# A DFT's maxima taken in passes, and the last token tiles split on VectorE: one change to a fused FNet and MLP kernel

## Chip, cores, metric

The kernel runs on one core of one Trainium2 chip. The metric is the device time of one execution in microseconds (us), the median of several runs. The core has TensorE (PE, with its weight loads PEld), VectorE (DVE), ScalarE (ACT), GpSimd (POOL) and SyncE (SP), which issues most DMAs.

## What is computed

```python
x = A_x                                    # 1 x 2048 x 576, f32
xn = _layernorm(x)                         # over the 576 columns
a, b = xn @ dft_hid_re.T, xn @ dft_hid_im.T
fourier = dft_seq_re @ a - dft_seq_im @ b  # dft_seq: 2048 x 2048
mlp = maximum(xn @ w1, 0) @ w2             # w1: 576 x 4608, w2: 4608 x 576
return x + fourier + mlp
```

All in float32. The kernel writes each f32 operand as a high and a low f16 part (`split`, or a copy and a subtraction) and multiplies high by high, high by low and low by high. The factors are scaled by powers of two, for which the kernel needs the largest absolute value of each matrix.

## The kernel before

**Tiles.** The 2048 tokens are 16 tiles of 128 rows and 4 groups of 512. The 4608 hidden columns are 9 blocks of 512. Most products are Strassen products in Winograd's form: 7 products instead of 8 for each 2 x 2 partition, which costs sums of blocks on VectorE ahead of and behind TensorE.

**The MLP** is a sequence of 36 steps, counted from 0: `steps[n]` is block n // 4 and group n % 4. Step n computes the first product of its block and group (`run`, L593 and L612 on TensorE) and the second product of the step before (`mlp2`, L699 on TensorE, L710 on ScalarE, L714 on VectorE). What `mlp2` has gathered in a sum buffer is added to a spill in DRAM by a DMA of GpSimd's queue (L717). From block 2 on, the order within a step is a list written out by hand, of which the change touches the entries `more` and `count`.

Two lists fill the gaps of the steps. `todo` holds the preparation of the next block: loads into a ring of two raw buffers, maxima, splits and sums, ten slots to a step (`work`). In the last block (steps 32 to 35) it holds the preparation of the DFT over the columns instead: `load_d(e)` loads one half of its matrix, `max_d` reduces it to a maximum per partition on VectorE (L161), `power_d` makes the scale, `split_d` (L229 on ScalarE, L230 on VectorE) and `sums_d` make the operands. Since the ring holds one half only, half 1 is loaded, reduced, then half 0 is loaded, reduced and split, and half 1 is loaded again. `passes` holds 64 loads of 512 KB of the sequence DFT's matrices into one staging buffer (`first_c`), each followed in the next pass by a sum of absolute values on ScalarE (`sum_c`, L1139). A step takes two passes, a step of group 1 three.

**The DFT over columns** has 8 steps (`for s in range(NS)`): TensorE's products (L1312), their sums, and `convert`, which makes the f16 operands R of four token tiles: copies on ScalarE (L1359, the high parts), subtractions for the low parts (L1363) and differences (L1367, L1375, L1376) on VectorE. Low parts of the later products (`a.start > 2`) are made by GpSimd.

**The last stage** multiplies the sequence DFT's matrices with R, in 16 units `(p, kh)`: p is one of 8 pairs of output tiles, kh says which half of the token tiles is summed over (kh = 0: tiles 0 to 7). Each unit has 7 products of 24 matmuls (L1555); VectorE adds each to the output in SBUF (L1561). An output starts as what the spill holds (`load_out`) and is stored after its kh = 1 unit. The operands of a unit come from four blocks of 512 KB (`load_c`, one unit ahead), with sums on VectorE (L1409 to L1414) and the split (L229, L230) three products ahead. The last 22 operations of `convert` (`rest_r`, two token tiles) are done during the first units, two after each product, their low parts by GpSimd.

TensorE, ScalarE, VectorE, GpSimd and SP each take their instructions in order; `tc.issue_after` puts an instruction behind another one on its engine. All five queues come from one scheduler that follows the order of the program where nothing is waited for.

Of the kernel before, what the change touches and what calls it, by code (L numbers as in the profile page):

```python
# [10 lines left out]
F32 = mybir.dt.float32  # L11
# [7 lines left out]
P = 128  # L19
S = 2048  # L20
D = 576
# [33 lines left out]
def kernel(  # L55
# [103 lines left out]
    def magnitude(dst, src):  # L159

        nc.vector.tensor_reduce(dst, src, AX.XY, ALU.max, apply_absolute_value=True)  # L161
# [61 lines left out]
    def cell(tag, n=NQ):  # L223
        return small.tile([P, n], F32, tag=f"c_{tag}", name=f"c_{tag}", bufs=2)
# [821 lines left out]
            owed.pop()  # L1046
            work(True)

    PARTS_D = (slice(0, 3), slice(3, KT))
    DK = 7  # L1050
    dspots = [dspot[0], w2spots[3][0], kspot[0] + DX + FW]
    dparts = [
# [13 lines left out]
    def load_d(e):  # L1066
        for j in (2 * e, 2 * e + 1):
            load_raw(("d", j), dft[:, :, j * EH : (j + 1) * EH], [P, KT, EH])

    def max_d(j, c):  # L1070

        if "d" not in mx:
            mx["d"] = cell("md", 8)
        k = 2 * j + c
        with tc.issue_after(order["vfree"]):
            magnitude(mx["d"][:, k : k + 1], raws["d", j][:, PARTS_D[c]])

    def power_d():
        m = cell("mdd", 1)
# [35 lines left out]

    NP = NT // 2
    HK = NT // 2
    units = [(0, 0), (1, 0), (1, 1), (0, 1)] + [(p, kh) for p in range(2, NP) for kh in range(2)]
    sums_c = const.tile([P, len(units), 4], F32, name="sums_c")
    firsts = {}  # L1120

# [12 lines left out]
    def sum_c(m):  # L1134

        n, q = divmod(m, 4)
        f = firsts.pop(m)
        with tc.issue_after(order.get("free", order["s"])):
            nc.scalar.activation(  # L1139
                f, f, AF.Abs, scale=2.0**-10, accum_out=sums_c[:, n, q : q + 1]  # L1140
            )


    passes = [
        lambda m=m: (sum_c(m - 1) if m else None, first_c(m)) for m in range(4 * len(units))
    ]
    passes.append(lambda: sum_c(4 * len(units) - 1))

    tq = itertools.chain(*(sums_x(g) for g in range(NG)))
    for n in range(2, len(steps)):  # L1150
        b, g = steps[n]
        pb, pg = steps[n - 1]
        if g == 0 and b:
            if b + 1 < NB:
                todo += prepare_block(b + 1)
            else:
                d = power_d()
                for e in (1, 0):
                    todo += [lambda e=e: load_d(e)] + [lambda: None] * 2
                    todo += [lambda j=j, c=c: max_d(j, c) for j in (2 * e, 2 * e + 1) for c in range(2)]  # L1160
                todo += [lambda: next(d), lambda: None, lambda: later(d)]
                todo += prepare_d(0) + [lambda: load_d(1), lambda: None] + prepare_d(1)[:DA]
        if b == 0 and g + 1 < NG:
            with tc.issue_after(order["lo"]):
                weave(stats([(g + 1) * TG + i for i in range(TG)]))
        if b == NB - 1 and g == 1:

            w = turn("w2s", w2spots)
            sumbufs[:] = [
                w[:, k : k + 2 * EH].rearrange("p (c e) -> p c e", e=EH)  # L1170
                for k in range(0, 6 * EH, 2 * EH)
            ]
        if b >= BB:
            run, rests = step_products(n)
            used = lambda q: run(q, True)
            m = lambda q: mlp2(pb, pg, q)
            end = lambda q: ends and ends.pop(0)()
            ready = lambda q: [work() for _ in range(q)]
            brief = lambda q: [work(True) for _ in range(q)]
            count = lambda q: passes and passes.pop(0)()  # L1180
            left = lambda q: n == 2 * NG and lates[-1][q]()
            t_sum = lambda q: next(tq, None)
            more = lambda q: g == 1 and count(q)
            rest = lambda q: rests(n + 1 if n + 1 < len(steps) else None)
            for do, q in (
                (run, P1), (left, 0), (run, P5), (end, 0), (end, 0), (m, 0), (brief, 1), (left, 1),
                (run, P6), (end, 0), (end, 0), (run, P2), (t_sum, 0), (m, 1), (used, P2), (more, 0), (ready, 1),
                (run, P7), (t_sum, 0), (ready, 1), (m, 2), (used, P7), (count, 0), (m, 3), (brief, 1),
                (rest, 0), (run, P3), (brief, 1), (m, 4), (used, P3), (t_sum, 0), (ready, 1),
                (run, P4), (used, P4), (t_sum, 0), (m, 5), (ready, 1), (count, 0),  # L1190
                (m, 6), (brief, 3),
            ):
                do(q)
            continue
        ps = []
        for i in range(NF):
            if n == 2:
                if i == 3:
                    mlp2(pb, pg, 0)
                    mlp2(pb, pg, 1)  # L1200
                ps.append(early.pop(0) if early else mlp1(b, g, i))
            else:
                if n == 3 and i == 0:
                    mlp2(pb, pg, 0)
                    mlp2(pb, pg, 1)
                with behind("pe" if n == 3 and i == 0 else None):
                    mlp1_step(b, g, i, ps)
            if n == 2:
                t = (g + 1) * TG + i
                normalize(t, after="free" if i == 3 else None)  # L1210
                remainder(t, nc.vector)
                transposes_dma(t, nc.scalar)
            if i % 2:
                after = ("w2hi", ("E", 15))[i // 2] if n == 2 else None
                lates.append(mlp1_out(
                    b, g, i // 2, *ps[i - 1 : i + 1], after=after,
                    late=i == 1 or n == 7 if b else n == 2,
                ))
                if n == 2 and i == 1:
                    lates[-1][0]()  # L1220
            if n > 2 and i == 1:
                gates[n - 2] = order["s"], order["lo"]
            if n == 2:
                if i > 1:
                    todo += prepare_block(1) if i == 2 else []
                    for _ in range(1 if i == 2 else 2):
                        work()
                continue
            if b:
                work()  # L1230
            for q in ((2,), (3,), (4, 5), (6,))[i] if n == 3 else range(2 * i, min(2 * i + 2, 7)):
                mlp2(pb, pg, q)
                if b:
                    if q in (3, 5):
                        lates[-1][q == 5]()
                    for _ in range((2, 0, 0, 5, 0, 0, 2)[q]):
                        next(tq, None)
                else:
                    for _ in range(2):
                        work()  # L1240
            for _ in range(1 + i % 2 if b else (2, 2, 2, 4)[i]):
                work()
            if (n, i) > (6, 1) and i % 2 and passes:
                passes.pop(0)()
        if n == 2:
            for q in range(2, 7):
                mlp2(pb, pg, q)
                if q == 2:
                    lates[-2][1](("E", 15))
                if q in (3, 5):  # L1250
                    lates[-1][q == 5]()

            gates[n - 2] = order["s"], order["lo"]
            for _ in range(9):
                work()
# [96 lines left out]
    def convert(s, k):  # L1352
# [6 lines left out]
            nc.scalar.activation(r[:, 0, a], x[:, b], AF.Copy)  # L1359

        def lo(a, b):
            tt = (nc.gpsimd if a.start > 2 or late_r else nc.vector).tensor_tensor
            tt(r[:, 1, a], x[:, b], r[:, 0, a], ALU.subtract)  # L1363

        def t13():
# [82 lines left out]
    for s in range(NS):  # L1448
        lows = [(s, 0, P4), (s, 0, P3), (s, 1, P4), (s, 1, P3)]
        lows += [(s, e, P2) for e in range(2)]  # L1450
        if s + 1 < NS:
            lows += [(s + 1, e, P5) for e in range(2)]
        end = s == NS - 1
        one, two = convert(s, 1), convert(s, 0)
        if s == 0:
            seq = (
# [49 lines left out]
        if s == 5:  # L1506
            load_c(0, [2, 3, 1])
    outs = {}
    ospots = [(dspots[1], o4 + 2 * W2W)[k] for k in (0, 1, 1, 0)]

    def load_out(p):
        o = outs[p] = words((ospots[p if p < 2 else 2 + p % 2], 4 * EH)).rearrange("p (h e) -> p h e", h=2)
        for h in range(2):
            g, c = divmod(p + h * NP, TG)
            for col in range(2):
                nc.sync.dma_start(o[:, h, col * EH : (col + 1) * EH], spill[g, c // 2, col][:, c % 2])

    psw.release()
    psd = [tc.alloc_tile_pool(name="psd0", bufs=4, space=PSUM, side="right")]
# [11 lines left out]
    AHEAD = 3  # L1531
    load_out(0)
    operand(2, False)
    late_r.append(True)
    keys = ("h1", "l1", "h2", "l2", "t13", "t2", "t4", "h3b", "l3b", "h3a", "l3a")
    rest_r = [d[k] for d in (old, late) for k in keys]
    for n, (p, kh) in enumerate(units):
        if n + 1 < len(units):
            load_c(n + 1)
        if n == 0:  # L1540
            load_out(1)
        elif n > 2 and kh and units[n + 1 :]:
            load_out(units[n + 1][0])
        for i, (q, rq, first, row, col) in enumerate(PRODUCTS):
            m = n * 7 + i
            if m + AHEAD < 7 * len(units):
# [14 lines left out]
            order["o"] = nc.vector.scalar_tensor_tensor(  # L1561
                o, ps, us["c"][:, n : n + 1], o, ALU.mult, ALU.add
            ).ins
            for _ in range(2):
                if rest_r:
                    rest_r.pop(0)()
            if kh and i in (2, 4, 5, 6):
# [58 lines left out]
```

## Time and profile before

| | |
|---|---|
| median of 3 runs | 1237.79 us (1235.23 to 1239.27) |
| the profiled execution | 1238.07 us, span 1235.9 us |
| TensorE busy | 1211.0 us (98% of the span) |
| VectorE busy | 999.4 us (81%) |
| ScalarE busy | 707.2 us (57%) |
| GpSimd busy | 210.2 us (17%) |
| granted TensorE clock | 1.00 |

A line of the waits names the engine and line that waited, the releaser, the total in us, how often, and the longest. A group has its count, then busy us and mean ns, then the idle time just ahead of it and what ended most of that. A line of a timeline has start, length, engine and line, and in brackets the idle time ahead of it.

### The profile page before, as it was taken

To read this page: it belongs to the slowest core of one execution; us is meant where nothing else is said; L and a number is where in the kernel's file an instruction comes from. 1 tells how busy PE (TensorE), PEld (TensorE's weight loads), DVE (VectorE), ACT (ScalarE), POOL (GpSimd) and SP (SyncE) were. 2 spreads that over 40 slices of the span, in tenths; PEclk is the share of its full clock that TensorE was granted. 3 is DMA by queue.
4 is the path that set the end of the run, shared out by engine and by line. 5 is a ranking of instruction groups with operands and counts; after the bars stand their busy time and mean duration, and the time that the engine had idled before them with its cause. 6 is when DMAs were issued, how large, how long until landed. Compare 5 with 4: busy or idle time off the path is not lost.

```text
span 1235.9 us, 24513 instructions
## 1 busy us (share of the span) xinstructions
PE 1211.0 (98%) x10173; PEld 956.2 (77%) x10173; DVE 999.4 (81%) x1619; ACT 707.2 (57%) x1073; POOL 210.2 (17%) x241
## 2 busy tenths in 40 slices
PE   8999999999999999999999999899989999999998
PEld 7665657888888788888888888677767777777777
DVE  8998899778877788778877877777798878787875
ACT  5655457677686666767766757656643333333332
POOL 2431211111121212111111111144440000000000
PEclk9999999999999999999999999999999999999999
DMA  8994545757566567567576686520243534433420
GB/s 316 210 159 99 85 70 134 150 122 161 136 136 155 138 143 154 119 152 145 120 161 155 136 195 128 104 30 1 69 158 110 168 112 137 142 126 125 134 88 20
DMA packets 82207, 160.80 MB, mean 130 GB/s; under 512 B 22320, under 2 KB 42544, under 8 KB 82096
## 3 DMA queue, kind: packets, MB, share of 16 engines
q1 hardware_dynamic: 59312, 116.77, 30.0%
q0 software_dynamic: 22784, 42.48, 23.9%
q8 instruction: 79, 1.29, 0.4%
q14 instruction: 32, 0.26, 0.1%
HBM read 108.10 MB, written 51.90 MB: 129 GB/s over the span
## 4 chain that ended last, share of the span: by engine, by line
PE 73%; DVE 15%; issue 5%; ACT 3%; DMA 3%; POOL 0%; SPq 0%; ACTq 0%; POOLq 0%; DVEq 0%
PE p L1555 24%; PE p L699 22%; PE bank L593 19%; DVE arena L230 3%; PE U L1312 3%; PE W L1312 2%; DMA arena<-in_w_dram 1%; PE p L392 1%; DVE arena L714 1%; PE bank L612 1%; ACT arena L229 1%; DVE arena L468 1%; DMA arena<-in_dft_dram 1%; PE V L1312 1%; DVE arena L451 1%
## 5 line engine op out<-in xcount | busy, mean ns | idle before, releaser
L699 PE MATMUL p<-arena 128*128 128x288 f16 x3024 | 400.2, 286 | 5.8 <-DVE arena L714 5.7
L699 PEld LDWEIGHTS <-arena 128*128 128x128 f16 x3024 | 295.8, 98 | 83.5 <-issue 8.4
L1555 PE MATMUL p<-arena 128*128 128x288 f16 x2688 | 330.2, 286 | 5.2 <-DVE arena L1561 4.7
L1555 PEld LDWEIGHTS <-arena 128*128 128x128 f16 x2688 | 263.0, 98 | 72.4 <-issue 6.3
L593 PE MATMUL bank<-arena 128*128 128x256 f16 x2580 | 304.8, 273 | 1.2 <-ACT arena L647 1.1
L593 PEld LDWEIGHTS <-arena 128*128 128x128 f16 x2580 | 250.1, 98 | 39.1 <-issue 7.6
L229 ACT ACTIVATE arena<-arena,sc_c 128x1024 f16<-128x1024 f32 x112 | 124.3, 1144 | 199.5 <-DVE arena L1410 75.3
L717 POOL DMA_DIRECT2D spill<-arena x144 | 128.6, 911 | 553.4 <-DVE arena L714 504.5
L230 DVE SCALAR_TENSOR_TENSOR arena<-arena,sc_c 128x1024 f16<-128x1024 f32 x112 | 144.3, 1312 | 51.8 <-ACT arena L229 51.8
L710 ACT ACTIVATE arena<-p,c_ub 128x576 f32<-128x576 f32 x144 | 105.5, 734 | 43.3 <-PE p L699 38.2
L230 DVE SCALAR_TENSOR_TENSOR arena<-arena,c_sw 128x640 f16<-128x640 f32 (+2 forms) x118 | 98.2, 847 | 24.8 <-ACT arena L229 24.5
L229 ACT ACTIVATE arena<-arena,c_sw 128x640 f16<-128x640 f32 (+3 forms) x118 | 90.3, 795 | 23.1 <-DVE c_sw L171 10.8
L628 DVE TENSOR_TENSOR arena<-arena 128x1024 f16<-128x1024 f32 x56 | 68.5, 1224 | 42.9 <-ACT arena L624 42.8
L392 PE MATMUL p<-arena 128*128 128x128 f16 (+1 forms) x680 | 98.5, 300 | 1.8 <-ACT arena L347 1.1
L714 DVE SCALAR_TENSOR_TENSOR arena<-p,c_ub,arena 128x576 f32<-128x576 f32 x108 | 87.4, 810 | 7.7 <-PE p L699 5.1
L1312 PEld LDWEIGHTS <-arena 128*128 128x128 f16 x738 | 71.6, 98 | 19.7 <-issue 1.9
L392 PEld LDWEIGHTS <-arena 128*128 128x128 f16 x680 | 52.3, 98 | 40.3 <-issue 3.8
L619 ACT ACTIVATE arena<-arena 128x512 f16<-128x512 f32 x56 | 35.2, 628 | 67.7 <-DVE arena L649 39.7
L1561 DVE SCALAR_TENSOR_TENSOR arena<-p,us_c,arena 128x288 f32<-128x288 f32 x112 | 57.5, 513 | 13.8 <-PE p L1555 13.4
L1139 ACT ACTIVATE arena<-arena 128x1024 f32<-128x1024 f32 x64 | 67.0, 1047 | 2.0 <-DMA arena<-in_cre_dram 1.0
L1363 POOL TENSOR_TENSOR arena<-arena 128x576 f16<-128x576 f32 (+1 forms) x36 | 52.1, 1460 | 60.2 <-ACT arena L1359 52.5
L624 ACT ACTIVATE arena<-arena 128x1024 f16<-128x1024 f32 x56 | 58.8, 1050 | 0.0
(151 smaller groups left out, 1119.7 us busy)
## 6 DMA issues: line engine op xcount, KB each, us to landing
spill<-arena POOLq DMA_DIRECT2D x144, 288.0 KB, 4.8
arena<-in_cre_dram SPq DMA_DIRECT2D x64, 512.0 KB, 4.2
arena<-in_cim_dram SPq DMA_DIRECT2D x64, 512.0 KB, 4.7
arena<-in_w_dram SPq DMA_DIRECT2D x17, 640.0 KB, 5.3
arena<-in_w_dram SPq DMA_DIRECT2D x18, 576.0 KB, 4.8
arena<-in_x_dram SPq DMA_DIRECT2D x16, 288.0 KB, 7.1
spill<-in_x_dram SPq DMA_DIRECT2D x16, 288.0 KB, 5.5
arena<-spill SPq DMA_DIRECT2D x32, 144.0 KB, 2.2
```

The source lines that it names most:

```text
L229: nc.scalar.activation(hi, src, AF.Copy, scale=s).ins,
L230: nc.vector.scalar_tensor_tensor(lo, src, s, hi, ALU.mult, ALU.subtract).ins,
L392: order["m1"] = nc.tensor.matmul(ps[:, cols], w1s[b, i // 2][:, hl, i % 2 * KT + k], xT[g][:, kx, cols], start=(start and n == 0), stop=(s ...
L593: nc.tensor.matmul(ps[:, i], l, r, start=first and i == m == 0, stop=m == len(todo) - 1, skip_group_check=not first or i > 0,)
L628: order["lo"] = nc.vector.tensor_tensor(lo, stage[:, 1 + 2 * i :][:, :2], hi, ALU.subtract).ins
L699: order["pe"] = nc.tensor.matmul(ps[:, c], h[:, x, qa, c * P : (c + 1) * P], w[:, y, qb], start=first and i == 0 and j == 0, stop=i == NQ ...
L710: freed(nc.scalar.activation(o, ps, AF.Copy, scale=us[b]))
L714: add = nc.vector.scalar_tensor_tensor(o, ps, us[b], o, ALU.mult, ALU.add)
L717: nc.gpsimd.dma_start(spill[g, row, col], o, accum_op=ALU.add)
L1139: nc.scalar.activation(f, f, AF.Abs, scale=2.0**-10, accum_out=sums_c[:, n, q : q + 1])
L1312: nc.tensor.matmul(ps, l, r, start=first and m == 0, stop=m == len(todo) - 1, skip_group_check=not first,)
L1555: nc.tensor.matmul(ps, w[:, a, k], r[:, c, RQ[rq]], start=first and k == 0 and j == 0, stop=k == HK - 1 and j == 2, skip_group_check=not f ...
```

## The change

The maxima of the DFT's column matrices are taken in six passes of 960 columns through the staging buffer of `passes`, in front of pass 24, by VectorE. Steps of group 3 now also take three passes. In the last block, half 0 is loaded and split at once and half 1 is loaded one time, four slots ahead of its first split.

The units of the last stage start with four of kh = 0 (p = 0 to 3), and then take kh = 1 of the same four. Two outputs in SBUF don't hold four, so those of p = 0 and 1 are written back to their spill after their first unit and read again. `late_r` is set at the last step of the DFT over columns, and its sense is turned: from there on all low parts are made by VectorE. The 22 operations of `rest_r` are handed out six to a unit.

```diff
+    ND = 6
+
+    def first_d(m):
+        if m == 0:
+            mx["d"] = const.tile([P, ND], F32, name="max_d")
+        n = KT * 2 * D // ND
+        f = firsts["d", m] = words(fspot, n)
+        with behind("loads"):
+            nc.sync.dma_start(f, dft.rearrange("p k e -> p (k e)")[:, m * n : (m + 1) * n])
+
-    def max_d(j, c):
...
+    def max_d(m):
+        f = firsts.pop(("d", m)).rearrange("p (a b) -> p a b", a=2)
         with tc.issue_after(order["vfree"]):
-            magnitude(mx["d"][:, k : k + 1], raws["d", j][:, PARTS_D[c]])
+            magnitude(mx["d"][:, m : m + 1], f)
...
-    units = [(0, 0), (1, 0), (1, 1), (0, 1)] + [(p, kh) for p in range(2, NP) for kh in range(2)]
+    units = [(p, 0) for p in range(4)] + [(p, 1) for p in range(3, -1, -1)] + [(p, kh) for p in range(4, NP) for kh in range(2)]
...
+    parts = [(first_c, sum_c, m) for m in range(4 * len(units))]
+    parts[24:24] = [(first_d, max_d, m) for m in range(ND)]
+
+    def part(k):
+
+        if k:
+            _, take, m = parts[k - 1]
+            take(m)
+        if k < len(parts):
+            load, _, m = parts[k]
+            load(m)
+
+    passes = [lambda k=k: part(k) for k in range(len(parts) + 1)]
...
                 d = power_d()
-                for e in (1, 0):
-                    todo += [lambda e=e: load_d(e)] + [lambda: None] * 2
-                    todo += [lambda j=j, c=c: max_d(j, c) for j in (2 * e, 2 * e + 1) for c in range(2)]
-                todo += [lambda: next(d), lambda: None, lambda: later(d)]
-                todo += prepare_d(0) + [lambda: load_d(1), lambda: None] + prepare_d(1)[:DA]
+                todo += [lambda: (load_d(0), next(d)), lambda: None, lambda: later(d)]
+                todo += prepare_d(0) + [lambda: load_d(1)] + [lambda: None] * 3 + prepare_d(1)[:DA]
...
-            more = lambda q: g == 1 and count(q)
+            more = lambda q: g % 2 and count(q)
...
-            tt = (nc.gpsimd if a.start > 2 or late_r else nc.vector).tensor_tensor
+            tt = (nc.gpsimd if a.start > 2 and not late_r else nc.vector).tensor_tensor
...
         end = s == NS - 1
+        if end:
+            late_r.append(True)
...
-    ospots = [(dspots[1], o4 + 2 * W2W)[k] for k in (0, 1, 1, 0)]
-
-    def load_out(p):
-        o = outs[p] = words((ospots[p if p < 2 else 2 + p % 2], 4 * EH)).rearrange("p (h e) -> p h e", h=2)
+    ospots = [dspots[1], o4 + 2 * W2W]
+
+    def load_out(p, back=False):
+        o = outs[p] = words((ospots[(p + (p > 3)) % 2], 4 * EH)).rearrange("p (h e) -> p h e", h=2)
...
-                nc.sync.dma_start(o[:, h, col * EH : (col + 1) * EH], spill[g, c // 2, col][:, c % 2])
+                part = o[:, h, col * EH : (col + 1) * EH], spill[g, c // 2, col][:, c % 2]
+                nc.sync.dma_start(*(part[::-1] if back else part))
...
-    late_r.append(True)
...
-        if n == 0:
-            load_out(1)
-        elif n > 2 and kh and units[n + 1 :]:
-            load_out(units[n + 1][0])
+        after = units[n + 1 : n + 2]
+        if n in (1, 2):
+            load_out(p - 1, True)
+        if after and after[0][0] != p and n != 4:
+            load_out(after[0][0])
...
-            for _ in range(2):
+            for _ in range((1, 0, 0, 1, 2, 2, 0)[i]):
                 if rest_r:
                     rest_r.pop(0)()
```

More of the change, by code (lines that the diff above doesn't have):

```diff
@@ L1047, in work @@
             work(True)
-    PARTS_D = (slice(0, 3), slice(3, KT))
     DK = 7
@@ L1068, in load_d @@
             load_raw(("d", j), dft[:, :, j * EH : (j + 1) * EH], [P, KT, EH])
-    def max_d(j, c):
-        if "d" not in mx:
-            mx["d"] = cell("md", 8)
-        k = 2 * j + c
+    ND = 6
[8 more added lines that the diff above has]
+        f = firsts.pop(("d", m)).rearrange("p (a b) -> p a b", a=2)
         with tc.issue_after(order["vfree"]):
-            magnitude(mx["d"][:, k : k + 1], raws["d", j][:, PARTS_D[c]])
+            magnitude(mx["d"][:, m : m + 1], f)
     def power_d():
@@ L1141, in sum_c @@
             )
[L1144 to L1147, printed above, removed]
+    parts = [(first_c, sum_c, m) for m in range(4 * len(units))]
[8 more added lines that the diff above has]
+    passes = [lambda k=k: part(k) for k in range(len(parts) + 1)]
     tq = itertools.chain(*(sums_x(g) for g in range(NG)))
```

## The prediction

> **What bounds the kernel now.** I read the page, then what TensorE waited for, then TensorE by stretches of time, then the timelines of the engines around each stretch with a gap.
>
> ```profile
> span 1235.9 us, 24513 instructions
> PE 1211.0 (98%) x10173; PEld 956.2 (77%) x10173; DVE 999.4 (81%) x1619; ACT 707.2 (57%) x1073; POOL 210.2 (17%) x241
> PE p L699 <- DVE arena L714: 5.7, 8, 1.9
> PE p L1555 <- DVE arena L1561: 4.7, 5, 1.5
> PE bank L612 <- DVE arena L649: 3.5, 2, 2.3
> PE p L1555 <- ACT arena L1348: 0.5, 1, 0.5
> ```
>
> TensorE is busy for 1211.0 of 1235.9 us and the change takes no matmul away, so it can only move the 24.9 us in which TensorE stands still. The waits (line, releaser, total, times, longest) show where the touched parts sit: 4.7 us in the last stage (L1555), behind VectorE's additions of L1561. The timelines put 1.07 us (L593) and 2.29 us of the 3.5 (L612) into the end of the MLP. Those 8.1 us are the most that the two aims can bring.
>
> ```profile
> L1555 PE MATMUL p<-arena 128*128 128x288 f16 x2688 | 330.2, 286 | 5.2 <-DVE arena L1561 4.7
> 895.00:905.00 10.00, 8.20 (x66) 6.27 (x65) 9.97 (x9) 5.90 (x9) 6.37 (x4) 1.00 0.87 289
> 905.00:915.00 10.00, 9.14 (x72) 7.03 (x72) 10.00 (x13) 6.20 (x7) 2.96 (x3) 1.00 0.32 111
> 915.00:925.00 10.00, 7.99 (x64) 6.25 (x64) 9.97 (x10) 1.94 (x3) 5.77 (x3) 1.00 0.32 104
> 960.00:970.00 10.00, 10.00 (x84) 7.99 (x82) 8.34 (x9) 2.45 (x3) 0.00 (x0) 1.00 0.42 129
> ```
>
> The first row is the last stage's matmuls: 330.2 us for 112 products, 2.95 us each. The others are stretches: length, then busy time of PE, weight load, DVE, ACT, POOL, then clock, DMA share and GB/s. The first unit and a half of the last stage are the only place where VectorE is full (29.9 of 30 us) and TensorE loses (4.7 us). Later VectorE needs 8.3 of 10 us, GpSimd does nothing, and TensorE loses nothing.
>
> **Low parts of the last token tiles.** Why VectorE is full there shows in the groups of 885 to 921 us (first three) and of 925 to 1200 us (the next two):
>
> ```profile
> L230 DVE SCALAR_TENSOR_TENSOR arena<-arena,sc_c 128x1024 f16<-128x1024 f32 x9 | 14.7, 1652 | 1.1 <-ACT arena L229 1.1
> L1363 POOL TENSOR_TENSOR arena<-arena 128x576 f16<-128x576 f32 x10 | 17.0, 1719 | 17.6 <-ACT arena L1359 17.6
> L1409 DVE TENSOR_TENSOR arena<-arena 128x1024 f32<-128x1024 f32 x1 | 2.3, 2295 | 0.0
> L230 DVE SCALAR_TENSOR_TENSOR arena<-arena,sc_c 128x1024 f16<-128x1024 f32 x94 | 118.3, 1282 | 46.4 <-ACT arena L229 46.4
> L1409 DVE TENSOR_TENSOR arena<-arena 128x1024 f32<-128x1024 f32 x13 | 15.8, 1215 | 0.0
> 883.79 1.13 DVE L1363 TENSOR_TENSOR arena<-arena 128x576 f16<-128x576 f32 x2 [1.36 <-ACT arena L1359]
> ```
>
> The same instruction takes 1282 ns while GpSimd rests and 1652 ns while it works. L230 alone pays 9 x 0.37 = 3.3 us; one L1409 takes 2295 ns, against 1215 later, so another 1.1; the shorter ones take it to an estimated 7 us. The change makes the 12 low parts that GpSimd did in this stretch (10 wide, 2 narrow) VectorE instructions: 4 in the last step of the DFT over columns, 8 in the four units. A wide and a narrow one took 1.13 us together on VectorE (last row), so about 0.7 each: 12 x 0.7 = 8.4 us. VectorE's work in all hardly changes (7 taken, 8.4 given). But only the 4 (about 3 us) must be done early. The other 8, and the differences of L1367 to L1376 between them, are handed out six operations to a unit, because the first four units now read only token tiles 0 to 7. Per unit of 7 products (7 x 2.95 = 20.6 us) VectorE has 20.6 x (1 - 0.834) = 3.4 us free and gets about 2. In the first 40 us it loses 7 us of slowed work and some 2 of moved differences and gets 3 + 1.2 of low parts: 38 of 40 us become about 33, the share at which TensorE loses nothing later.
>
> What is late next: the 0.5 us behind L1348 stays (ScalarE empties PSUM). A product that adds to an older bank needs L1561 of two products before, and after two extra operations in a row VectorE catches up late; I leave 0.8 us for that. Term: 4.7 - 0.8 = **3.9 us gained**. Bounds: 4.7 if nothing stays; 2.0 if each of the four units keeps some 0.7 us, since 2 of the 3.4 us free go in clumps.
>
> Here a rule of the Trainium skill stands against the row. SBUF — State Buffer, section "Who interferes with whom", says that a VectorE instruction with two SBUF inputs and a GpSimd one that reads SBUF exclude each other, for the whole instruction. By it the delay would be up to 12 x 1.7 = 20 us (an estimate from GpSimd's row) instead of 7. The trace shows partial delays; the stall to be gained is 4.7 us either way.
>
> **Order of units and the write-back.** Two partial outputs (4 DMAs of 144 KB each) go back to their spill and are read again, all on SP's queue. Behind the write-back, which waits for L1561 of the unit's last product, stand the reload and the next column loads. The reload is used a whole unit (20.6 us) later, the loads about half a unit later; single loads land in 4 to 11 us (rows below). I take 0. If that cover went, a unit would wait for the landing beyond it, at most about 2 us each, twice.
>
> **DFT loads at the end of the MLP.** Before, the second half of the DFT's matrix is loaded a third time one slot ahead of its use, and ScalarE waits for it:
>
> ```profile
> 767.97 0.55 SPq L141 DMA_DIRECT2D arena<-in_dft_dram  x1
> 770.92 1.01 ACT L229 ACTIVATE arena<-arena,c_sd 128x864 f16<-128x864 f32 x1 [3.46 <-DMA arena<-in_dft_dram]
> 778.64 0.78 ACT L229 ACTIVATE arena<-arena,c_sd 128x576 f16<-128x576 f32 x1 [2.55 <-DMA arena<-in_dft_dram]
> 775.19 1.47 PE L593 MATMUL bank<-arena 128*128 128x256 f16 x12 [1.07 <-ACT arena L647]
> 782.04 0.40 PE L612 MATMUL bank<-arena 64*128 64x256 f16 x4 [2.29 <-DVE arena L649]
> 737.39 0.19 ACT L1139 ACTIVATION_READ_ACCUMULATOR arena<-arena 128x1 f32 x1
> 745.38 2.35 ACT L229 ACTIVATE arena<-arena,c_sd 128x864 f16<-128x864 f32 x3
> 747.64 0.57 ACT L645 ACTIVATE arena<-bank 128x512 f32<-128x512 f32 x1
> ```
>
> ScalarE's copies that free PSUM (L645 to L648) queue behind, then VectorE's L649, then TensorE: 1.07 + 2.29 = **3.4 us that go** in step 35 (steps count from 0; the last block is 32 to 35). With the maxima out of the list, the 12 slots in front of the splits vanish, and by the count of ten slots a step the splits of the first half take step 32 from slot 3, the second load slot 3 of step 33, its first three splits slots 7 to 9 of step 33. Those are the slots of the 745.38 row.
>
> What is new there. (1) SP issues that load behind the pass's own load, and that waits for its sum on ScalarE (737.39 + 0.19 in step 33), so about 738.3 with the maxima's pushes. 512 + 720 + 720 KB go one after the other. In the old place the last piece landed 778.64 - 767.97 = 10.7 us after its issue with the same three in flight: here 749, while the third split wants it at 747. At TensorE, 0 to 2.3 us; I take 0.5, since the second piece goes out 2 us closer to the first than before. If every piece landed in the 2 us plus bytes over 436 GB/s of the Trainium skill (DMA: Bandwidth & Descriptors, "Anatomy of one DMA"), all three would be there after an estimated 6.6 us and this item would be 0; the landings in this trace are longer. (2) The split of rows 15 and 16 now lands in slot 9 of step 32. Its low part overwrites a sum buffer that step 32's last product has just sent to the spill:
>
> ```profile
> 723.63 1.84 POOL L717 DMA_DIRECT2D spill<-arena  x2 [2.03 <-DVE arena L714]
> spill<-arena POOLq DMA_DIRECT2D x3, 288.0 KB, 6.6
> 730.77 1.23 DVE L628 TENSOR_TENSOR arena<-arena 128x1024 f16<-128x1024 f32 x1 [1.55 <-ACT arena L624]
> 732.51 0.81 DVE L714 SCALAR_TENSOR_TENSOR arena<-p,c_ub,arena 128x576 f32<-128x576 f32 x1
> 733.30 3.10 PE L699 MATMUL p<-arena 128*128 128x288 f16 x24
> ```
>
> The second of these DMAs starts at 724.55 and lands 6.6 us later: 731.1. VectorE stands still until then and has the split, another split (0.8 and 1.1), L628, L646 and L714 to do: L714 ends at about 735.5 instead of 733.3, and the second product of the last row starts at 734.8. I take 0.8 us (0 to 1.6). Together this part: 3.4 - 0.5 - 0.8 = **2.1 us gained**, from 3.4 to -0.5.
>
> **Maxima in passes.** The eight reductions go from steps 32 and 33, where they cost nothing:
>
> ```profile
> 700.00:740.00 40.00, 40.00 (x352) 33.20 (x351) 29.34 (x40) 24.83 (x40) 7.25 (x9) 1.00 0.84 196
> L161 DVE TENSOR_REDUCE c_md<-arena 128x1 f32<-128x864 f32 (+1 forms) x8 | 7.2, 895 | 0.0
> 713.52 1.04 DVE L161 TENSOR_REDUCE c_md<-arena 128x1 f32<-128x864 f32 x1
> ```
>
> Six of 960 columns come, 1.04 + 96/960 = about 1.1 us each. Counting passes (3 before step 8, then 10 per block), they fall into steps 17 (three), 18 (two) and 19 (one). New is that VectorE waits for a load which goes out only when the maximum before it is done. Step 17 in the old trace:
>
> ```profile
> 396.40 0.68 DVE L649 TENSOR_TENSOR arena<-bank,arena 128x512 f32<-128x512 f32 x1
> 397.73 0.61 PE L612 MATMUL bank<-arena 64*128 64x256 f16 x8
> 400.81 0.75 DVE L230 SCALAR_TENSOR_TENSOR arena<-arena,c_sw 128x512 f16<-128x512 f32 x1 [1.94 <-ACT arena L229]
> 403.47 0.81 DVE L714 SCALAR_TENSOR_TENSOR arena<-p,c_ub,arena 128x576 f32<-128x576 f32 x1
> 402.81 3.15 PE L699 MATMUL p<-arena 128*128 128x288 f16 x24
> arena<-in_cre_dram SPq DMA_DIRECT2D x1, 512.0 KB, 3.9
> arena<-in_cim_dram SPq DMA_DIRECT2D x1, 512.0 KB, 7.8
> ```
>
> The first maximum stands ahead of L649: it ends 1.1 us later, at 398.2, and L612 wants to start at 397.73: 0.5 us. The load behind it goes out at 397.2 and lands in 3.9 us (the load of this step at 399.6): 401.1, while VectorE, idle from 398.9 before, is there at 400.0. The maximum, the split of 400.81, L650, ScalarE's answer and L632 follow, and L714 ends at 405.6 instead of 404.3; TensorE, itself 0.5 late, needs it at 404.8: 0.8 us. The third, behind a weight load (the 7.8 us row), may reach into step 18: 0.5. Step 18 has VectorE idle where its two fall; step 19 repeats the first case: 0.4. Together **2.2 us lost**, 0.4 (order luckier, landings short) to 5 (every landing 7.8 us). The sums that move to the fourth step of a block are 1 us of ScalarE each, on an engine that is 57% busy: 0.
>
> **Sum.** -3.9 - 2.1 + 2.2 = -3.8 us. The profiled execution took 1238.07 us, 2.2 us around its span: 1234.3. The median shown is 1237.79, 0.28 lower: **1234.0**. A measurement of this kernel can tell about 0.3% (3.7 us) from no change, so the forecast lies right on that bound, at 1234.1.
>
> **Rivals.**
> - *All covers hold* (0.15): the maxima find gaps, the loads land. -4.3 - 3.4 + 0.4 = -7.3: 1230.5. For it: eight reductions cost nothing at 700 to 740. Against it: VectorE had no load to wait for there in the passes' rhythm.
> - *The DFT wait only changes place* (0.18): ScalarE is held by the second load in step 33 (2.3 at TensorE), the sum buffer costs 1.6, the passes 2.5, the units 0.9 more. -3.0 + 0.5 + 2.5 = 0: 1237.8. For it: 10.7 us of landing, and only four slots between issue and use.
> - *VectorE is stopped by the passes' loads* (0.15), the slower side. Where a load lands after about 5 us the maximum comes too late, and it decides from about 8 us on for the second, third and fifth pass: at 8.5 us they hold VectorE for 5, 4 and 2 us, and TensorE nearly as long, since L714 stands behind; with 2 us from the pushes, 13 instead of 2.2: +7, 1244.8 at the worst and 1241.5 with half of it. For it: the 7.8 us row; against it: most such loads land in about 4 us.
> - That the change doesn't do what it says is excluded by the listing: the flag is set before step 7's low parts are issued, and 71 passes fit 73 slots.
>
> **How the numbers follow.** The forecast has 0.52, its own range 1231 to 1236.5; about six tenths of it lies below 1234.1. Faster by over 0.3%: 0.15 + 0.32 = 0.47 and a little of the second rival, 0.49. Slower: 0.15. Same: 0.36. The range leaves out the worst half of the slower rival and the best of the first: 1229.8 to 1240.5.
>
> **What would show it.** Right: no POOL group of L1363 after about 885 us, L230 near 1.28 us throughout, TensorE's wait for L1561 at 1 us or less; no ScalarE wait for the DFT's loads in the last step; reductions of 960 columns in steps 17 to 19 with small gaps at L612 and L699. Wrong: VectorE waiting several us for those loads, ScalarE held in step 33, gaps in units 1 to 4, or a wait for the reloaded outputs.

## The result and the profile after

| | before | after |
|---|---|---|
| median us (9 runs each, taken together) | 1237.85 | 1232.97 |
| lowest and highest | 1235.23, 1239.27 | 1230.92, 1234.5 |
| the profiled execution, its span | 1238.07, 1235.9 | 1233.90, 1232.1 |

The ratio is 0.9959 (95%: 0.9947 to 0.9970). The kernel is 4.9 us faster, which is a little over the 0.3% that can be told from no change. The forecast was 1234.0, 1.0 us too slow.

The page of the kernel after: its head, then the lines of what TensorE waited for (line, releaser, total us, times, longest).

```profile
span 1232.1 us, 24558 instructions
PE 1211.8 (98%) x10173; PEld 957.2 (78%) x10173; DVE 999.3 (81%) x1629; ACT 707.8 (57%) x1073; POOL 189.6 (15%) x229
PE p L699 <- DVE arena L714: 6.6, 8, 2.1
PE bank L612 <- DVE arena L649: 1.2, 1, 1.2
PE p L1570 <- DVE arena L1576: 0.4, 1, 0.4
```

L1570 and L1576 are the last stage's matmul and addition (L1555 and L1561 before). Their wait fell from 4.7 to 0.4 us, the wait behind ScalarE's L1348 is gone, L612 lost its 2.29 us, and the MLP's wait for L714 grew from 5.7 to 6.6. Adding up every gap of TensorE by stretches of each trace gives this (the gaps of the timeline, in us; "both" is the sum of the two rows where the maxima and the DFT's loads lie):

| stretch | before | after | change | predicted |
|---|---|---|---|---|
| 300 to 460 (maxima in passes) | 2.17 | 2.41 | +0.24 | +2.2 |
| 700 to 820 (end of the MLP) | 3.53 | 2.98 | -0.55 | -2.1 |
| both | 5.70 | 5.39 | -0.31 | +0.1 |
| 893 to the end (last stage) | 5.17 | 0.38 | -4.79 | -3.9 |
| the rest | 10.36 | 10.36 | 0 | 0 |

In all the gaps fell by 5.1 us and the median by 4.9.

The stretches of the last stage after (length; busy us of PE, weight load, DVE, ACT, POOL; clock, DMA share, GB/s):

```profile
895.00:905.00 10.00, 10.00 (x83) 7.89 (x82) 10.00 (x11) 5.60 (x8) 0.00 (x0) 1.00 0.83 271
905.00:915.00 10.00, 10.00 (x84) 7.99 (x82) 10.00 (x15) 5.83 (x7) 0.00 (x0) 1.00 0.77 250
915.00:925.00 10.00, 10.00 (x83) 7.88 (x82) 10.00 (x14) 3.35 (x4) 0.00 (x0) 1.00 0.30 94
```

TensorE now runs through: 10.00 of 10 us in each, where it had 8.20, 9.14 and 7.99. But VectorE is still full, 30.0 of 30 us. The prediction had it fall to 33 of 40.

### The profile page after: what moved, and what is told of

It reads as the page before. It is cut to its first block, busy times and chain, and to the rows that moved or that the text cites. A ratio compares the mean times of both kernels' runs of the same rounds, so it can differ in the third digit from the quotient of the medians.

```text
span 1232.1 us, 24558 instructions
## 1 busy us (share of the span) xinstructions
PE 1211.8 (98%) x10173; PEld 957.2 (78%) x10173; DVE 999.3 (81%) x1629; ACT 707.8 (57%) x1073; POOL 189.6 (15%) x229
## 4 chain that ended last, share of the span: by engine, by line
PE 66%; DVE 18%; issue 7%; ACT 4%; DMA 4%; POOL 1%; SPq 0%; ACTq 0%; POOLq 0%; DVEq 0%
PE p L1570 24%; PE p L699 19%; PE bank L593 16%; DVE arena L230 3%; PE U L1324 3%; PE W L1324 2%; DMA arena<-in_w_dram 1%; PE p L392 1%; DVE arena L714 1%; DMA spill<-arena 1%; DVE arena L468 1%; ACT arena L229 1%; PE bank L612 1%; DVE c_mf L161 1%; DVE arena L628 1%
## 5 line engine op out<-in xcount | busy, mean ns | idle before, releaser
L1570 PE MATMUL p<-arena 128*128 128x288 f16 x2688 | 329.9, 286 | 0.4 <-DVE arena L1576 0.4
L1570 PEld LDWEIGHTS <-arena 128*128 128x128 f16 x2688 | 263.0, 98 | 67.1 <-issue 0.7
L230 DVE SCALAR_TENSOR_TENSOR arena<-arena,sc_c 128x1024 f16<-128x1024 f32 x112 | 140.9, 1281 | 47.7 <-ACT arena L229 47.7
L628 DVE TENSOR_TENSOR arena<-arena 128x1024 f16<-128x1024 f32 x56 | 68.5, 1223 | 42.3 <-ACT arena L624 42.1
L714 DVE SCALAR_TENSOR_TENSOR arena<-p,c_ub,arena 128x576 f32<-128x576 f32 x108 | 87.4, 810 | 8.4 <-PE p L699 5.6
L1576 DVE SCALAR_TENSOR_TENSOR arena<-p,us_c,arena 128x288 f32<-128x288 f32 x112 | 57.5, 513 | 13.8 <-PE p L1570 13.4
L1324 PE MATMUL U<-arena 128*128 128x288 f16 x400 | 55.8, 286 | 0.0
```

Of the source, the lines that this page charges most:

```text
L230: nc.vector.scalar_tensor_tensor(lo, src, s, hi, ALU.mult, ALU.subtract).ins,
L628: order["lo"] = nc.vector.tensor_tensor(lo, stage[:, 1 + 2 * i :][:, :2], hi, ALU.subtract).ins
L714: add = nc.vector.scalar_tensor_tensor(o, ps, us[b], o, ALU.mult, ALU.add)
L1324: nc.tensor.matmul(ps, l, r, start=first and m == 0, stop=m == len(todo) - 1, skip_group_check=not first,)
L1570: nc.tensor.matmul(ps, w[:, a, k], r[:, c, RQ[rq]], start=first and k == 0 and j == 0, stop=k == HK - 1 and j == 2, skip_group_check=not f ...
```

## Experiments

Each was timed in several rounds beside the kernel before. The question first was which part of the change brings the 4.9 us, and within the last stage whether it is the engine of the low parts or their spread.

**Part by part.** e1 has the whole change of the last stage (unit order, write-back, low parts, spread) and the MLP of before; e2 has the MLP's change alone.

```
e1:  hunks from `tt = ...` and `late_r` to `range((1, 0, 0, 1, 2, 2, 0)[i])` on the kernel before
e2:  hunks first_d, max_d, parts, passes, todo, more on the kernel before
```

> The change to the last stage alone (order of units, write-back, low parts on VectorE, six operations to a unit); the maxima stay as before. Theory A (the gain comes from the last stage): TensorE's waits there fall from 5.2 us to about 0.4, the waits of the DFT's loads at the end of the MLP stay (3.4 us); 1237.85 - 4.8 = 1233.0 us. Rival B (both parts bring about half): gaps of some 2.5 us stay in the first units, 1235.5 us.

> The maxima in passes alone; the last stage stays as before. Theory A: the 3.4 us behind the loads of the DFT's matrix go, 2.7 us behind the sum buffer's DMA come in step 33, the passes cost about nothing: 1237.85 - 0.5 = 1237.3 us, the waits for L1561's successor stay at 4.7 us. Rival B: about 1235.5 us. The working of the prediction (2.1 gained, 2.2 lost) would give 1237.7.

e1: 1232.41 beside 1238.23, ratio 0.9950 (0.9938 to 0.9963). e2: 1238.95, ratio 1.0007 (0.9996 to 1.0017). The waits of e1 and then of e2:

```profile
PE p L1558 <- DVE arena L1564: 0.4, 1, 0.4
PE bank L612 <- DVE arena L649: 3.8, 2, 2.6
```

```profile
PE p L1567 <- DVE arena L1573: 4.7, 5, 1.5
738.60 1.63 PE L699 MATMUL p<-arena 128*128 128x288 f16 x12 [2.09 <-DVE arena L714]
```

The last stage is the whole gain. The maxima and the earlier load bring nothing: e2 loses the old gap at L612, but has 2.09 us behind L714 in step 33 (second line, a row of its timeline), which the kernel after has as well.

**The engine or the spread.** e3 is the kernel after with low parts on VectorE, but the old order of units and two operations after each product. e4 is the kernel after with the new order and spread, but low parts on GpSimd.

```diff
e3, against after:
-            for _ in range((1, 0, 0, 1, 2, 2, 0)[i]):
+            for _ in range(2):
     (units, ospots, load_out and the loop's loads as before)
e4, against after:
-            tt = (nc.gpsimd if a.start > 2 and not late_r else nc.vector).tensor_tensor
+            tt = (nc.gpsimd if a.start > 2 or late_r else nc.vector).tensor_tensor
     (late_r set where it was before)
```

> The whole change, but with the old order of units and two operations after each product, so that VectorE has all low parts to do in the first two units. Theory S (the early work is what counts: 7.5 us of slowed instructions go, 8.4 us of low parts come, VectorE stays full for 39 of 40 us): 3 to 5 us of TensorE's waits stay in the first two units, about 1236.5 us. Rival C (GpSimd's slowing of VectorE is all): waits of 1 us or less, about 1233 us.

> The whole change, but the low parts stay where they were (GpSimd), now spread over four units. Theory S: VectorE's slowed instructions (about 7 us) are spread over 80 us in which it has some 14 us free: waits of 1 to 2 us, about 1234.5 us, L230 still above 1.4 us on the mean in these units. Rival C: the waits of 4 to 5 us stay, about 1237 us.

e3: 1233.07 beside 1238.23, ratio 0.9961 (0.9948 to 0.9973). e4: 1239.54, ratio 1.0008 (0.9997 to 1.0018). The engine is all of it; writing the operations over four units brings nothing. e3's only gap of TensorE in the first units, and one of its stretches:

```profile
934.49 65.70 PE L1568 MATMUL p<-arena 128*128 128x288 f16 x535 [0.39 <-DVE arena L1574]
905.00:915.00 10.00, 10.00 (x83) 7.99 (x82) 10.00 (x15) 6.89 (x7) 0.00 (x0) 1.00 0.68 210
```

e4 has the wait of before to the tenth:

```profile
PE p L1569 <- DVE arena L1575: 4.7, 5, 1.5
```

Why it brings nothing shows in the last low part of the kernel after (first) and of e3 (second):

```profile
930.77 0.75 DVE L1375 TENSOR_TENSOR arena<-arena 128x576 f16<-128x576 f32 x1
```

```profile
930.87 0.74 DVE L1375 TENSOR_TENSOR arena<-arena 128x576 f16<-128x576 f32 x1
```

Handed out over four units (82 us) or over two, they are done at the same time, less than two units in. The two kernels differ in the order of the program here; in the queue that VectorE got only a few neighbours change places. So it is in e4: GpSimd's last four low parts, then the same of the kernel before:

```profile
911.25 7.92 POOL L1375 TENSOR_TENSOR arena<-arena 128x576 f16<-128x576 f32 x4 [7.04 <-ACT arena L1371]
```

```profile
912.85 7.92 POOL L1363 TENSOR_TENSOR arena<-arena 128x576 f16<-128x576 f32 x4 [7.04 <-ACT arena L1359]
```

The scheduler appears to pull each operation forward once its inputs are there; the rows show the places, not the scheduler's reasons. In no run did the operations really run over four units, so what that would bring is not shown. e2 and e4 took 1 to 3 us longer than the nearest of their expectations, and no gap shows why (5.17 and 5.19 us in the last stage, 5.17 before); the runs of each spread over more than 5 us.

**The smallest edit.** e6 is the kernel before with nothing but the engine of the low parts. e7 adds to it four more empty slots behind the third load of the DFT's half 1, without any change to the maxima.

```diff
e6, against before:
-            tt = (nc.gpsimd if a.start > 2 or late_r else nc.vector).tensor_tensor
+            tt = (nc.gpsimd if a.start > 2 and not late_r else nc.vector).tensor_tensor
...
         end = s == NS - 1
+        if end:
+            late_r.append(True)
e7, beside that:
-                todo += prepare_d(0) + [lambda: load_d(1), lambda: None] + prepare_d(1)[:DA]
+                todo += prepare_d(0) + [lambda: load_d(1)] + [lambda: None] * 5 + prepare_d(1)[:DA]
```

> The kernel before, with nothing but the low parts on VectorE from the last step of the DFT over columns on: old order of units, two operations after each product, no write-back, maxima as before. Theory C (GpSimd's slowing of VectorE is all): TensorE's waits in the last stage fall from 5.2 to about 0.4 us, as with the whole of that part: 1232.4 to 1233 us. Rival S (the order of units and the spread carry part): 2 us or more stay, 1235 us and above.

> As the run before, and in the last block five empty slots instead of one between the third load of the DFT's half and its first split; the maxima stay as before. If the 3.4 us (2.8 in the run of the last stage alone) are nothing but the lead of that load, they go without any pass: 1237.85 - 4.8 - 3.0 = 1230.0 us. Rival: the splits then fall on the last slots of step 35 and on the tail of the list in the DFT, and 2 us come back there: 1232 us.

e6: 1233.02 beside 1238.12, ratio 0.9961 (0.9947 to 0.9974): these few lines give what the whole change gives. e7: 1228.76, ratio 0.9928 (0.9915 to 0.9940), faster than both kernels: 4.2 us below the kernel after's median. The second piece of the third load goes out when it did before (first row, SP's timeline: 768.20, before 767.97), but ScalarE's first splits of half 1 come 8.7 us later (779.64, before 770.92) and no longer wait (second row). The third row is TensorE's one gap from 700 to 800:

```profile
768.20 0.55 SPq L141 DMA_DIRECT2D arena<-in_dft_dram  x1
779.64 2.33 ACT L229 ACTIVATE arena<-arena,c_sd 128x864 f16<-128x864 f32 x3
787.77 1.63 PE L699 MATMUL p<-arena 128*128 128x288 f16 x12 [0.54 <-DVE arena L714]
```

So the waits of step 35 (3.4 us before, 2.6 in e6) go without moving a maximum: not by an earlier load, but by a later use of it. e10 puts the same empty slots on e1.

> The whole change to the last stage (order of units, write-back, six operations to a unit, low parts on VectorE), maxima as before, and five empty slots between the third load of the DFT's half and its first split. If the order of units, the write-back and the spread neither bring nor cost anything, it stands with the run that had only the low parts and the early load: 1228.8 us. Rival: the 2.4 MB of write-back and reload cost 1 to 2 us, 1230 to 1231 us.

e10: 1229.13 beside 1237.71, ratio 0.9936 (0.9923 to 0.9948), within e7's interval. The order of units and the write-back thus neither give nor take anything that can be told. In the profiles the slots are worth 2.1 us of gaps from 700 to 820 (3.19 in e6, 1.10 in e7) and 1.9 in e10 against e1 (2.82, 0.94); the medians fell by 4.3 and 3.3. Where the rest of that comes from is not shown; single runs of one kernel differ by as much (2.5 us in e1's).

**The wait for the sum buffer.** In step 33 of the kernel after VectorE stands still for 3.68 us. e5 is the kernel after with the split of rows 15 and 16, which overwrites the buffer, put behind that of rows 11 and 12.

```diff
+        rest = [(7, 9, 1), (15, 7, 2), (8, 0, 3), (11, 3, 2), (13, 5, 2)]
+        if e == 0:
+            rest.insert(3, rest.pop(1))
...
-            + pieces((7, 9, 1), (15, 7, 2), (8, 0, 3), (11, 3, 2), (13, 5, 2))
+            + pieces(*rest)
```

> The whole change, with one split of the DFT's first half (rows 15 and 16) two slots later, in step 33. Theory D (VectorE's 3.7 us in step 33 are its wait for the sum buffer's DMA to the spill): that wait and TensorE's 2.7 us behind it go, 1232.97 - 2.7 = 1230.3 us. Rival E (VectorE is behind there anyway, or the next load then comes later): a gap of 2 us stays in step 33 or 34, 1232.5 us.

e5: 1231.72 beside 1238.12, ratio 0.9948 (0.9936 to 0.9961). The gaps of step 33 are gone, but one of 1.12 us came behind ScalarE:

```profile
750.45 3.00 PE L593 MATMUL bank<-arena 128*128 128x256 f16 x26 [1.12 <-ACT arena L645]
745.39 1.06 ACT L1148 ACTIVATE arena<-arena 128x1024 f32<-128x1024 f32 x1 [2.83 <-DMA arena<-in_cre_dram]
```

ScalarE waits there 2.83 us for a load of the passes. The gaps of 700 to 820 went from 2.98 to 1.68. So theory D holds for VectorE's wait and the 2.7 us behind it, and rival E in part: a wait for the next load came. The median is 1.25 us lower, and the two ratios' intervals overlap, so the cause is shown by the gap, not by the time.

**GpSimd beside VectorE.** e8 is the kernel after with idle work for GpSimd: beside each late low part on VectorE it subtracts the high part from itself into a buffer that nobody reads.

```diff
             tt(r[:, 1, a], x[:, b], r[:, 0, a], ALU.subtract)
+            if late_r:
+                for k in range(a.start, a.stop):
+                    nc.gpsimd.tensor_tensor(junk_r, r[:, 0, k], r[:, 0, k], ALU.subtract)
```

> The whole change, and GpSimd subtracts each high part from itself into a scratch tile, 288 columns at a time, whenever VectorE makes a low part: nothing waits for it. Theory C: VectorE's instructions with two inputs in SBUF slow down again (L230 from 1.28 to 1.5 us or more in the first two units), TensorE's waits for VectorE's additions come back to 3 to 5 us, 1237 us. Rival F (the gain comes from what had to be waited for, not from GpSimd's use of SBUF): waits of 1 us or less, 1233 us.

e8: 1241.54 beside 1238.12, ratio 1.0028 (1.0018 to 1.0037): 8.6 us above the kernel after, and slower than before, by work that nothing waits for. Groups from 885 to 945 us of e8, then the same of the kernel after (count, busy us, mean ns, idle time ahead):

```profile
L1379 POOL TENSOR_TENSOR junk_r<-arena 128x288 f16<-128x288 f16 x25 | 28.3, 1132 | 27.6 <-ACT arena L1372 26.0
L230 DVE SCALAR_TENSOR_TENSOR arena<-arena,sc_c 128x1024 f16<-128x1024 f32 x16 | 21.3, 1347 | 0.0
L1376 DVE TENSOR_TENSOR arena<-arena 128x576 f16<-128x576 f32 x12 | 12.0, 1020 | 1.4 <-ACT arena L1372 1.4
L1580 DVE SCALAR_TENSOR_TENSOR arena<-p,us_c,arena 128x288 f32<-128x288 f32 x12 | 6.0, 503 | 0.0
```

```profile
L230 DVE SCALAR_TENSOR_TENSOR arena<-arena,sc_c 128x1024 f16<-128x1024 f32 x18 | 22.7, 1280 | 0.8 <-ACT arena L229 0.7
L1375 DVE TENSOR_TENSOR arena<-arena 128x576 f16<-128x576 f32 x12 | 8.9, 754 | 1.5 <-ACT arena L1371 1.4
L1576 DVE SCALAR_TENSOR_TENSOR arena<-p,us_c,arena 128x288 f32<-128x288 f32 x15 | 7.7, 514 | 0.4 <-PE p L1570 0.4
```

VectorE's low part goes from 754 to 1020 ns and its split from 1280 to 1347, while the addition from PSUM stays (514, 503). The split was expected at 1500 or more; the delay fell more on the low parts. TensorE's waits come back:

```profile
PE p L1574 <- DVE arena L1580: 4.2, 4, 1.9
PE U L1340 <- DVE arena L1358: 2.9, 3, 1.5
```

From 893 us on its gaps are 6.65 us, where the kernel after has 0.38: 6.3 of the 8.6 us. Where the rest comes from is not shown. e8 has the low parts and the slowed instructions both on VectorE, so 8.6 us is not what GpSimd's work cost in the kernel before.

**What the maxima cost.** e9 is the kernel after without the six loads and reductions.

```diff
-    parts[24:24] = [(first_d, max_d, m) for m in range(ND)]
+    mx["d"] = const.tile([P, ND], F32, name="max_d")
+    nc.vector.memset(mx["d"], 1.0)
```

> The whole change, but the six loads and reductions of the maxima are left out and the constant 1 stands in their place; the rest of the passes stays, earlier by six. If the passes cost what the prediction gave them, 1232.97 - 2.2 = 1230.8 us. By the trace of the whole change, whose gaps in steps 16 to 19 add up to 2.7 us against 2.2 us before, they cost 0.5 us: 1232.5 us.

e9: 1230.41 beside 1237.71, ratio 0.9941 (0.9928 to 0.9955). That is 2.6 us under the kernel after, with overlapping intervals. Its gaps from 300 to 460 are no smaller (2.31, after 2.41); from 700 to 820 they are 1.35 instead of 2.98, all of it in step 33:

```profile
736.71 1.63 PE L699 MATMUL p<-arena 128*128 128x288 f16 x12 [1.35 <-DVE arena L714]
731.09 0.82 DVE L230 SCALAR_TENSOR_TENSOR arena<-arena,c_sd 128x576 f16<-128x576 f32 x1 [2.00 <-DMA spill<-arena]
```

So where they are taken the maxima cost nothing that the gaps show; taken out, VectorE's wait for the sum buffer is 2.00 instead of 3.68 us, another landing of the same DMA (5.5 us after its start, in the kernel after 7.2). In the kernel after the passes run six longer, and one of their loads goes out just ahead of that DMA:

```profile
724.02 0.33 SPq L1138 DMA_DIRECT2D arena<-in_cim_dram  x1
```

In e9 SP issues no load between 717 and 738 us. This load may be what holds the DMA up; no run changes it alone. Whether the other 1.0 us of the medians is the maxima's stays open.

## Why the prediction was right, and where not

**Low parts: direction and size right, one reason wrong.** Predicted was 3.9 us (bounds 4.7 and 2.0); the stretch brought 4.79, just past the upper bound, because the 0.5 us behind L1348 went too, where the prediction let it stay. The step "38 of 40 us become about 33" failed: VectorE is as full as before, and the spread by which the prediction got there does not reach the queue (e3, e4). That the term still came out near is in part luck. What held is the other half of the same step, that VectorE's instructions run undisturbed. The groups of 885 to 921 us after:

```profile
L230 DVE SCALAR_TENSOR_TENSOR arena<-arena,sc_c 128x1024 f16<-128x1024 f32 x9 | 11.4, 1280 | 0.0
L1375 DVE TENSOR_TENSOR arena<-arena 128x576 f16<-128x576 f32 x10 | 7.4, 754 | 1.5 <-ACT arena L1371 1.4
```

1652 ns became 1280, and a wide low part costs 754 ns, near the 0.7 taken. So VectorE can be full in these units and cost TensorE nothing, with the additions and splits that TensorE needs in time; that this is because the low parts among them can wait is a reading that no run tests alone. Counting its busy share, as the prediction did, can't tell the two cases apart; the lateness of L1561 can.

**The rule on exclusion was set aside too quickly.** The prediction read the 20 us by the rule and the 7 by the trace as a disagreement. The row below is from the groups of the kernel before, 885 to 921 us: the addition with one input in PSUM took 507 ns, three of the five while GpSimd worked, no more than the 514 of the kernel after. The instructions with two SBUF inputs were slowed, and in e8 again. That agrees with the section "Who interferes with whom" of the Trainium skill's SBUF — State Buffer, by which a VectorE instruction with at most one SBUF input, outside the modes that use both ports, is not disturbed. The delay of some 7 us over 12 low parts is about 0.6 us each, an estimate that would fit an exclusion where the later one waits for the rest of the other; no run here measured single pairs.

```profile
L1561 DVE SCALAR_TENSOR_TENSOR arena<-p,us_c,arena 128x288 f32<-128x288 f32 x5 | 2.5, 507 | 0.0
```

**Order of units and write-back: 0, right.** TensorE never waits for the reload, and e10 and e7 can't be told apart.

**DFT loads: 3.4 us went, but more came back than predicted.** Nothing of step 35's waits is left. For the second load 0.5 us was taken; TensorE lost 0.24 there (last row), but ScalarE was late by its wait for a load of the passes (the row above it), and the splits of half 1 had no wait for theirs. The fit that the prediction set beside these landings (Trainium skill, DMA: Bandwidth & Descriptors, "Anatomy of one DMA") is given there for DMAs of GpSimd's queue; these go out from SP's. The sum buffer was the mis-sized term: 0.8 taken, 1.6 at most, and 0.65 + 2.09 = 2.74 measured. Rows of the kernel after, from the timelines of GpSimd, VectorE, TensorE and ScalarE:

```profile
725.96 1.75 POOL L717 DMA_DIRECT2D spill<-arena  x2 [1.80 <-DVE arena L714]
734.01 0.82 DVE L230 SCALAR_TENSOR_TENSOR arena<-arena,c_sd 128x576 f16<-128x576 f32 x1 [3.68 <-DMA spill<-arena]
738.65 0.81 DVE L714 SCALAR_TENSOR_TENSOR arena<-p,c_ub,arena 128x576 f32<-128x576 f32 x1
736.02 1.40 PE L699 MATMUL p<-arena 128*128 128x288 f16 x10 [0.65 <-DVE arena L628]
739.51 1.63 PE L699 MATMUL p<-arena 128*128 128x288 f16 x12 [2.09 <-DVE arena L714]
748.89 1.06 ACT L1145 ACTIVATE arena<-arena 128x1024 f32<-128x1024 f32 x1 [1.73 <-DMA arena<-in_cre_dram]
753.96 3.00 PE L593 MATMUL bank<-arena 128*128 128x256 f16 x26 [0.24 <-ACT arena L645]
```

The mechanism is the predicted one, down to the instructions behind it. The landing came about 7.2 us after the second DMA's start (6.6 taken), and the work behind it on VectorE delayed L628 and L714, so that TensorE was stopped twice, where the prediction counted one stop.

**Maxima: 2.2 us predicted, 0.2 measured in gaps.** VectorE's, ScalarE's and TensorE's rows of step 17 and the start of step 18:

```profile
397.63 1.15 DVE L161 TENSOR_REDUCE max_d<-arena 128x1 f32<-128x960 f32 x1
399.29 0.87 PE L612 MATMUL bank<-arena 64*128 64x256 f16 x8
403.26 1.15 DVE L161 TENSOR_REDUCE max_d<-arena 128x1 f32<-128x960 f32 x1 [1.42 <-DMA arena<-in_dft_dram]
406.45 1.63 PE L699 MATMUL p<-arena 128*128 128x288 f16 x12 [0.19 <-DVE arena L714]
411.57 1.15 DVE L161 TENSOR_REDUCE max_d<-arena 128x1 f32<-128x960 f32 x1
413.70 0.83 ACT L229 ACTIVATE arena<-arena,c_sw 128x640 f16<-128x640 f32 x1 [3.68 <-DVE c_sw L171]
417.63 1.47 PE L593 MATMUL bank<-arena 128*128 128x256 f16 x12 [0.94 <-ACT arena L647]
```

VectorE did wait for the second load (1.42 us; 1.1 by the prediction), and a reduction takes 1.15 us (1.1 taken). But L612 has no gap, though its eight matmuls take 0.87 us instead of 0.61, and L714 costs 0.19 instead of 0.8. The prediction kept the old order of VectorE's queue behind the maximum; in the trace L714 stands ahead of L632 (405.59 and 406.37 us), where it had stood behind it and behind ScalarE's answer. The third maximum does cost something, 0.94 us where 0.5 was taken: it stands ahead of the scale of the next block's weights, ScalarE's split waits for that, and L647 and TensorE behind it. All six traces with these maxima have this gap (0.87 to 0.94), none of the other six. In return step 18's gaps behind L714, 1.06 and 0.52 us before, are 0.61 together. From 386 to 460 us the gaps are 1.74 us, against 2.17 before and 1.57 in e9: net, the maxima cost nothing to speak of in their own steps.

The other 0.67 us of the table's 2.41 is a gap at 342.89, ahead of the first maximum. All seven kernels whose steps of group 3 take three passes lose 0.64 to 1.18 us between 340 and 364, e9 without maxima too, and the other five 0 or 0.18. For these moved sums the prediction took 0; what in them makes the gap is not traced here.

Two errors with opposite signs (the maxima 2.0 us too dear, the end of the MLP 1.6 too cheap) mostly cancelled. That the time came out nearer than its terms is luck. The rival "the DFT wait only changes place" is what happened in the MLP, by the sum buffer more than by a load.

## What to carry to other kernels

Where a GpSimd operation of SBUF operands runs beside a full VectorE, price what it does to VectorE's instructions with two SBUF inputs, not only what it takes off VectorE: here moving the work back won 5 us although VectorE stayed full. Spreading operations in the program changed nothing here, where the queues came out the same; look where they land in the trace. And before a load's work is rebuilt to free a wait, try a few more slots between the load and its first use: that gave more here than the maxima's whole move.

## What was not expected of the hardware

In the stretches compared, only VectorE's instructions with two SBUF inputs were slowed beside GpSimd: the split by 29% in the kernel before (1282 to 1652 ns), the low part by 35% in e8 (754 to 1020), the addition from PSUM not at all. In four of the twelve profiled executions (after, e1, e8, e9) the granted clock fell for 10 to 20 us, at places from 10 to 910 us; e8 shows one in the row below, a stretch like those above: clock 0.83, third number from its end. By that clock it is worth about 1.7 us (an estimate: 0.17 of 10 us). Whether such dips make the runs of one kernel differ is not shown.

```profile
895.00:905.00 10.00, 8.62 (x58) 5.99 (x58) 10.00 (x10) 6.17 (x9) 7.60 (x7) 0.83 0.52 149
```
